# Attention after a long convolution: the residual added on VectorE, one paced list of background work, and two spectra loaded early

## The chip, the cores and the metric

The kernel runs on one core of a Trainium2 chip. The metric is device microseconds of one execution; the figure given is the median of several runs. TensorE (PE in the profile, with PEld for its weight loads) multiplies, VectorE (DVE), ScalarE (ACT) and GpSimd (POOL) work on elements, SyncE (SP) issues most DMAs. Matrix products land in PSUM and must be copied out by VectorE or ScalarE.

## What is computed

The state x has 2048 rows of 512 (bf16). Four layers follow each other, each on a layer norm of x and each added to x:

```
x = A_u
x = x + conv(layernorm(x))        # per channel: FFT convolution with a kernel made from the A, B, C parameters, plus a skip
x = x + attention(layernorm(x))   # 32 heads of 16; each row sees itself and 7 earlier rows, 2 apart
x = x + conv(layernorm(x))        # the same convolution
x = x + attention(layernorm(x))   # the same weights
```

The attention, cut to what matters:

```python
idx = pos[:, None] - arange(8)[None, :] * 2          # dilated window, masked where idx < 0
logits = einsum("bhsd,bhswd->bhsw", q, kg) * scale
o = einsum("bhsw,bhswd->bhsd", softmax(logits), vg)
return o.reshape(B, S, D) @ wo
```

## The kernel before, in words

**Stages.** `kernel_and_first_conv` builds the convolution's spectra, uses them for the first convolution and stores each of the four (one per 128 channels, 1 MB) to a DRAM scratch `kt_dram`. Then `b_layer` does the first attention, `a_layer` the second convolution, which loads the spectra `Kt` back (L731 to L734, two buffers), and `b_layer` the second attention, whose results go to the output. All share x as one tile `X` in SBUF.

**How the attention is tiled.** Since the window has a step of 2, even and odd rows are independent; `par` (0 or 1) names the half. With the half `fp` of the heads it makes four quarters, n = 2 par + fp. A quarter has two groups of 128 features, `f2` = 0 and 1, and nine blocks `b` of 114 queries (128 keys each).

- `start(g)` (L856): layer norm of four row slots on VectorE, transposes on PE, and four copies of the result from PSUM into `xnT` (L870, two on VectorE, two on ScalarE). Groups 0 and 1 make the even half, 2 and 3 the odd half.
- `proj(n, k)` (L875): one half (`h`) of the queries or keys of one `f2`: four matmuls of 512 columns, a copy to `st` (L886, VectorE for h = 0, ScalarE for h = 1) and, after the second half, two DMAs that spread `st` into a query or key set (`QS`, `KS`, L890). There are two pairs of sets, used by turns by the quarters. The order in k is f2, then query or key, then half: k = 0 to 3 is the whole of f2 = 0.
- `vproj(par, b)` (L892): the values of a block, four matmuls and a VectorE copy to `V` (L897).
- `logits(n, b)` (L899): 16 small matmuls for keys by queries of a block in two PSUM tiles `S4`, and two exponentials on ScalarE (L911) into one of three tiles `PT`.
- `values(n, b)` (L916): 16 matmuls of PT by V, whose extra column gives the sum; VectorE takes the reciprocal (L928) and multiplies (L930).
- `turn_o(n, b)` (L936): two transposes on PE; after every third block a VectorE copy to `oT` (L945).
- `out(m)` (L947): for one of 16 row slots four matmuls of `oT` by `wo` (L952), a fifth with the identity that adds the old x (L954), and a ScalarE copy to `X` (L955). After every fourth slot come the next layer norm's statistics (first attention: L202, L207 to L210 with a square root on ScalarE) or the store of the output (second attention).

The main loop (L974) takes t = 0 to 39. In step t it emits the logits of block t (t = 9 n + b), then background work, then the values of block t - 2, then the turn of block t - 4. The background work is: a value projection in the quarters n = 0 and 2, a projection of the next quarter's heads for b < 8 in n = 0, 1, 2, an `out` of the even rows for b < 8 in n = 3. All eight projections of quarter 0 are emitted before `start(2)` and the loop, the last eight outs after it.

All PSUM tiles but `S4` come from one pool of four (`psG`). The order in which an engine gets its instructions is that of a scheduler: it goes by the order of the code (with the earlier places that `at(tc, marks[..])` gives), and takes a later instruction when an earlier one isn't ready in its own reckoning. Waits are set from the data and buffers. Each engine then runs its list in order.

Of the kernel before, what the change touches and what calls it, by code (L numbers as in the profile page):

```python
# [11 lines left out]
ALU = mybir.AluOpType  # L12
AX = mybir.AxisListType
F32 = mybir.dt.float32
BF = mybir.dt.bfloat16
# [20 lines left out]
UF = 8  # L36
UP = UF + S // 2 + 16
NQ = 114
NB = 9
# [677 lines left out]
def a_layer(nc, tc, C, X, kt_dram, ln, ln_b, marks):  # L717

    with ExitStack() as es:
# [3 lines left out]
        kp = es.enter_context(tc.tile_pool(name="a_kt", bufs=2))  # L723
# [6 lines left out]
        Kt = []  # L730
        for dc in range(4):  # L731
            t = kp.tile([128, 4, 2, 512], BF, name="Kt", tag="Kt")
            nc.sync.dma_start(t[:], kt_dram[dc])
            Kt.append(t)  # L734
# [94 lines left out]
def b_layer(nc, tc, C, X, Wt, ln_b, marks, store=None, ln_next=None):  # L829

    with ExitStack() as es:
# [9 lines left out]
        oT = big.tile([128, 4, 2, QW], BF, name="oT")  # L841
# [14 lines left out]
        def start(g):  # L856
            par, j0 = g // 2, (g % 2) * 4
            xn = []
            for i in range(4):
                xn.append(xnp.tile([128, D], BF, name="xn", tag="xn"))  # L860
                ln_b.norm(xn[i][:], X[:, slot(g * 4 + i), :], g * 4 + i)
            for ch in range(2):
                pt = gps([128, 4, 2, 128], BF)
                for i in range(4):
                    for c in range(2):
                        ct = ch * 2 + c
                        nc.tensor.transpose(pt[:, i, c, :], xn[i][:, ct * 128:(ct + 1) * 128], ident[:])  # L867
                for c in range(2):
                    dst = xnT[:, ch * 2 + c, par, UF:UF + 1024].rearrange("c (p j) -> c p j", j=8)[:, :, j0:j0 + 4]
                    (nc.vector.tensor_copy if ch == 0 else nc.scalar.copy)(  # L870
                        dst, pt[:, :, c, :].rearrange("c j p -> c p j"))
# [3 lines left out]
        def proj(n, k):  # L875
# [10 lines left out]
            (nc.scalar.copy if h else nc.vector.tensor_copy)(st[n][:, h * 512:h * 512 + 512], ps[:])  # L886
# [12 lines left out]
        def logits(n, b):  # L899
            KS, QS = sets[n % 2]  # L900
            pt = PT[(n * NB + b) % 3]
            for ih in range(2):
                S4 = psS.tile([128, 2, 512], F32, name="S4", tag="S4")
                for sl in range(4):
                    f2, e = sl // 2, sl % 2
                    for ii in range(2):
                        r = slice(32 * (ih * 2 + ii), 32 * (ih * 2 + ii) + 32)
                        nc.tensor.matmul(S4[:, ii, sl * NQ:(sl + 1) * NQ], KS[r, e, f2, b * NQ + 1:b * NQ + 1 + NK],  # L908
                                         QS[r, e, f2, UF + b * NQ:UF + b * NQ + NQ],
                                         start=True, stop=True, skip_group_check=True)  # L910
# [3 lines left out]
        pts = {}  # L914

        def values(n, b):  # L916
            par, fp = n // 2, n % 2
            pt = PT[(n * NB + b) % 3]
            O = gps([128, 16, DH + 1])
            for i in range(4):  # L920
                for sl in range(4):
                    f2, e = sl // 2, sl % 2
                    c0 = (i * 4 + sl) * NQ
                    nc.tensor.matmul(O[:, f2 * 8 + i * 2 + e, :], pt[:, c0:c0 + 128],  # L924
# [7 lines left out]
            return on  # L932

        ons = {}

        def turn_o(n, b):  # L936
            par, fp = n // 2, n % 2
            if b % 3 == 0:
                pts[n] = gps([128, 3, 2, NQ], BF)
            on = ons.pop((n, b))  # L940
            for f2 in range(2):
                nc.tensor.transpose(pts[n][:, b % 3, f2, :], on[0:NQ, f2 * 128:(f2 + 1) * 128], ident[0:NQ, 0:NQ])  # L942
            if b % 3 == 2:
                dst = oT[:, fp * 2:fp * 2 + 2, par, (b - 2) * NQ:(b + 1) * NQ].rearrange("f t (b q) -> f t b q", q=NQ)
                nc.vector.tensor_copy(dst, pts[n][:].rearrange("f b t q -> f t b q"))  # L945

        def out(m):  # L947
            j = slot(m)
            par, jp = j % 2, j // 2
            ps = gps([128, 512])  # L950
            for ft in range(4):
                nc.tensor.matmul(ps[:], oT[:, ft, par, 0:1024].rearrange("f (p j) -> f j p", j=8)[:, jp],  # L952
                                 wo_t[:, ft, :], start=(ft == 0), stop=False)
            nc.tensor.matmul(ps[:], ident[:], X[:, j, :], start=False, stop=True)  # L954
            nc.scalar.copy(X[:, j, :], ps[:])  # L955
# [11 lines left out]
        for k in range(8):  # L967
            proj(0, k)
# [3 lines left out]
        todo = []  # L972
        LA, LT = 2, 4
        for t in range(4 * NB + LT):  # L974
            if t < 4 * NB:
                n, b = t // NB, t % NB
                logits(n, b)
                if n % 2 == 0:
                    vproj(n // 2, b)
                if n < 3 and b < 8:  # L980
                    proj(n + 1, b)
                if n == 3 and b < 8:
                    out(b)
            if t >= LA and t - LA < 4 * NB:
                n, b = (t - LA) // NB, (t - LA) % NB
                ons[n, b] = values(n, b)
            if t >= LT:
                turn_o((t - LT) // NB, (t - LT) % NB)
# [6 lines left out]
def kernel(  # L995
# [32 lines left out]
    marks = b_layer(nc, tc, C, X, Wt, ln_b, marks, ln_next=ln)  # L1028
    marks = a_layer(nc, tc, C, X, kt_dram, ln, ln_b2, marks)
# [33 lines left out]
```

## Time and profile before

| | |
|---|---|
| median of 4 runs (lowest to highest) | 587.9 us (582.4 to 589.48) |
| the profiled execution's own time | 587.12 us |
| its span | 585.3 us |
| busy: PE, DVE, ACT, POOL | 420.4, 425.6, 374.3, 17.9 us |
| first convolution with the spectra | to about 271 us |
| first attention | about 272 to 391 us |
| second convolution | about 390 to 461 us |
| second attention | about 461 to 585 us |
| granted TensorE clock, mean over the span | 0.9 |

A row of the timeline reads: start, duration, engine, line of the kernel, operation, written and read tiles with shapes, number of instructions merged; in brackets the idle time of the engine before it and what ended it. Durations of matmuls are modelled and overlap, so starts are the surer part. A shape such as 128x512 is partitions by elements.

### The profile page before, as it was taken

How to read it: one execution, taken by the hardware profiler on the slowest of the kernel's cores; microseconds unless marked ns; L12 is line 12 of the kernel's file. 1: busy time of each engine (PE TensorE's matmuls, PEld its weight loads, DVE VectorE, ACT ScalarE, POOL GpSimd, SP SyncE). 2: the span in 40 equal slices, each digit the busy share in tenths (PEclk: the TensorE clock that was granted, in tenths of full speed). 3: DMA queues.
4: the chain of work that ended last, by engine and by line, in shares of the span. 5: the costliest groups of instructions: out<-in, count | busy, mean ns of one | idle time of the engine just before them, and what ended most of it. 6: DMA issues, size and time to landing. Idle time of an engine off the chain costs nothing.

```text
span 585.3 us, 15269 instructions
## 1 busy us (share of the span) xinstructions
PE 420.4 (72%) x6522; PEld 261.4 (45%) x6522; DVE 425.6 (73%) x966; ACT 374.3 (64%) x511; POOL 17.9 (3%) x56
## 2 busy tenths in 40 slices
PE   1101576685684594636999999985997599989996
PEld 0101342462372363314455555643665445555573
DVE  5999999899999988336755565672999964545531
ACT  4999455363562453533488878954995448876793
POOL 0000000000000000321000000000000200000000
PEclk9999997796896887775999999996999789997999
DMA  8101146535535536571111110025661011111113
GB/s 291 76 1 36 25 106 90 107 112 109 93 120 109 69 122 130 125 197 73 73 47 47 56 56 20 3 91 125 173 175 14 1 73 42 52 56 37 39 46 101
DMA packets 80616, 48.57 MB, mean 83 GB/s; under 512 B 66723, under 2 KB 72740, under 8 KB 79268
## 3 DMA queue, kind: packets, MB, share of 16 engines
q1 hardware_dynamic: 77764, 42.75, 28.2%
q0 software_dynamic: 1200, 4.46, 2.7%
q8 instruction: 51, 0.84, 0.6%
q10 hardware_dynamic: 1584, 0.39, 0.3%
q14 instruction: 17, 0.14, 0.1%
HBM read 18.22 MB, written 8.39 MB: 45 GB/s over the span
## 4 chain that ended last, share of the span: by engine, by line
PE 35%; DVE 9%; ACT 7%; DMA 5%; issue 3%; SPq 0%; ACTq 0%; DVEq 0%
PE psG L884 10%; PE S L908 5%; PE psG L895 5%; PE psG L952 4%; PE psG L924 3%; ACT PT L911 3%; DMA zt<-Z 3%; DMA KS<-st 2%; DVE ln_st_b L202 2%; PE psG L867 1%; DVE pa L772 1%; DVE pb L773 1%; ACT xc L764 1%; PE psG L942 1%; PE psG L954 1%
## 5 line engine op out<-in xcount | busy, mean ns | idle before, releaser
L911 ACT ACTIVATE PT<-S 128x912 bf16<-128x912 f32 x144 | 126.4, 938 | 32.0 <-PE S L908 31.7
L884 PE MATMUL psG<-xnT,wqk 128*128 128x512 bf16 x256 | 70.6, 400 | 1.1 <-DVE xnT L870 1.1
L908 PE MATMUL S<-QS,KS 32*128 32x114 bf16 x1152 | 43.9, 213 | 5.8 <-DMA KS<-st 4.0
L928 DVE RECIPROCAL rd<-psG 114x16 f32<-114x16 f32 x72 | 18.2, 253 | 40.9 <-PE psG L924 40.9
L924 PEld LDWEIGHTS <-PT 128*128 128x128 bf16 x1152 | 39.2, 96 | 16.6 <-ACT PT L911 1.3
L897 DVE CAST V<-psG 128x512 bf16<-128x512 f32 x36 | 25.0, 694 | 24.3 <-PE psG L895 24.3
L924 PE MATMUL psG<-V,PT 128*128 128x17 bf16 x1152 | 41.0, 171 | 0.9 <-ACT PT L911 0.6
L254 PE MATMUL psA<-X,sb_F 128*128 128x128 bf16 x128 | 13.8, 242 | 36.4 <-ACT X L627 35.2
L895 PE MATMUL psG<-wv,xnT 128*128 128x512 bf16 x144 | 39.6, 389 | 0.0
L908 PEld LDWEIGHTS <-KS 32*128 32x128 bf16 x1152 | 26.1, 94 | 29.2 <-issue 16.1
L952 PE MATMUL psG<-wo_t,oT 128*128 128x512 bf16 x128 | 37.3, 400 | 0.3 <-DVE oT L945 0.2
L884 PEld LDWEIGHTS <-wqk 128*128 128x128 bf16 x256 | 23.5, 101 | 29.0 <-issue 5.1
L254 PEld LDWEIGHTS <-sb_F 128*128 128x128 bf16 x256 | 16.7, 105 | 42.7 <-issue 40.6
L886 DVE CAST st<-psG 128x512 bf16<-128x512 f32 x32 | 22.0, 687 | 17.0 <-PE psG L884 15.8
L272 PE MATMUL psA<-zt,sb_C 128*128 128x512 bf16 x30 | 15.2, 540 | 26.7 <-DMA zt<-Z 22.6
L241 ACT CAST Z<-psA 128x1024 bf16<-128x1024 f32 (+1 forms) x32 | 28.9, 977 | 7.1 <-PE psA L254 7.1
L584 PE MATMUL psk<-Ytab,Xtab 128*32 128x64 bf16 x1024 | 23.4, 205 | 12.9 <-issue 6.2
L930 DVE TENSOR_TENSOR on<-psG,rd 114x256 bf16<-114x256 f32 x72 | 30.1, 419 | 1.6
L587 PE MATMUL psk<-Y2tab,Xtab 128*32 128x48 bf16 x1024 | 22.5, 201 | 11.7 <-issue 9.9
L565 DVE TENSOR_TENSOR Ytab<-Ytab,MA 128x2048 bf16<-128x2048 bf16 (+1 forms) x33 | 30.6, 927 | 0.2
L567 DVE TENSOR_TENSOR Y2tab<-Ytab,MB 128x2048 bf16<-128x2048 bf16 (+1 forms) x33 | 30.5, 925 | 0.0
L241 ACT CAST xc<-psA 128x1024 bf16<-128x1024 f32 x16 | 15.7, 1014 | 22.4 <-PE psA L275 22.4
(183 smaller groups left out, 1013.4 us busy)
## 6 DMA issues: line engine op xcount, KB each, us to landing
kt_scratch<-Kt SPq DMA_DIRECT2D x4, 1024.0 KB, 3.9
QS<-st SPq DMA_DIRECT2D x32, 128.0 KB, 2.1
KS<-st SPq DMA_DIRECT2D x32, 128.0 KB, 2.1
Kt<-kt_scratch SPq DMA_DIRECT2D x4, 1024.0 KB, 5.9
X<-in_A_u_dram SPq DMA_DIRECT2D x4, 512.0 KB, 5.2
Xr<-in_A_u_dram SPq DMA_DIRECT2D x4, 512.0 KB, 4.7
out_dram<-X SPq DMA_DIRECT2D x4, 512.0 KB, 2.9
k_scratch<-KTq SPq DMA_DIRECT2D x7, 256.0 KB, 2.2
```

The lines of the kernel that those rows point to most:

```text
L241: self.nc.scalar.copy(dst, src)
L254: nc.tensor.matmul(o, F1[:, j, r, :], rhs_j(j), start=True, stop=not dk)
L565: nc.vector.tensor_tensor(v(Y[:, :, :, q * EYB:(q + 1) * EYB, :]), src, vm(self.mult(self.MA, lev, hc, EYB)), ALU.mult)
L567: nc.vector.tensor_tensor(v(Y2[:, :, :, (q - 1) * EYB:q * EYB, :]), src, vm(self.mult(self.MB, lev, hc, EYB)), ALU.mult)
L884: nc.tensor.matmul(ps[:], wqk[:, ct, f0:f0 + 128], xnT[:, ct, par, UF + h * 512:UF + h * 512 + 512], start=(ct == 0), stop=(ct == 3))
L895: nc.tensor.matmul(ps[:].rearrange("p h d -> p (h d)"), xnT[:, ct, par, NQ * b + 1:NQ * b + 1 + NK], wv[:, ct, :], start=(ct == 0), stop=( ...
L897: nc.vector.tensor_copy(V[:, par * NB + b, :, 0:DH], ps[:])
L908: nc.tensor.matmul(S4[:, ii, sl * NQ:(sl + 1) * NQ], KS[r, e, f2, b * NQ + 1:b * NQ + 1 + NK], QS[r, e, f2, UF + b * NQ:UF + b * NQ + NQ], ...
L911: nc.scalar.activation(pt[:, ih * 8 * NQ:(ih + 1) * 8 * NQ].rearrange("k (i x) -> k i x", i=2), S4[:, :, 0:4 * NQ], ACT.Exp, scale=DH ** -0.5)
L924: nc.tensor.matmul(O[:, f2 * 8 + i * 2 + e, :], pt[:, c0:c0 + 128], V[:, par * NB + b, (fp * 2 + f2) * 8 + i * 2 + e, :], start=True, stop ...
L930: nc.vector.tensor_tensor(on[0:NQ].rearrange("q (h d) -> q h d", d=DH), O[0:NQ, :, 0:DH], rd[0:NQ].unsqueeze(2).to_broadcast([NQ, 16, DH]) ...
L952: nc.tensor.matmul(ps[:], oT[:, ft, par, 0:1024].rearrange("f (p j) -> f j p", j=8)[:, jp], wo_t[:, ft, :], start=(ft == 0), stop=False)
```

## The change

In both attentions:

- A step t now takes two neighbouring blocks of one `f2` (over the nine steps of a quarter: the nine blocks of f2 = 0, then those of f2 = 1), where it took one block of both. The fifth step of a quarter has block 8 of f2 = 0 and block 0 of f2 = 1. `oT` is laid out by par first, and a turn writes one flat stretch of it.
- Only the first four projections (f2 = 0) stand before `start(2)`. The other 28 projections, the 18 value projections and the first eight outs, 54 pieces in all, form one list; a function `pace(t)` says how many of them are to be emitted by step t, linear between given points.
- `out`: 12 of 16 slots add the old x on VectorE from PSUM, without the fifth matmul. The odd ones of the last eight keep the matmul and the ScalarE copy.
- Copies to `st`: all on VectorE but those with h = 1 of quarter 0. Copies to `xnT`: groups 0 and 1 all on ScalarE; groups 2 and 3 half on each.

Around them: the pool of `Kt` is opened once, ahead of the first attention, and the loads of the first two spectra are emitted in the first attention at step 9. `a_layer` loads the other two.

```diff
-def a_layer(nc, tc, C, X, kt_dram, ln, ln_b, marks):
+def a_layer(nc, tc, C, X, kt_dram, kp, Kt, ln, ln_b, marks):
...
-        kp = es.enter_context(tc.tile_pool(name="a_kt", bufs=2))
...
-        Kt = []
-        for dc in range(4):
+        for dc in range(2, 4):
             t = kp.tile([128, 4, 2, 512], BF, name="Kt", tag="Kt")
             nc.sync.dma_start(t[:], kt_dram[dc])
             Kt.append(t)
...
-        oT = big.tile([128, 4, 2, QW], BF, name="oT")
+        oT = big.tile([128, 2, 4, QW], BF, name="oT")
...
-                    (nc.vector.tensor_copy if ch == 0 else nc.scalar.copy)(
+                    (nc.scalar.copy if par == 0 or c == 0 else nc.vector.tensor_copy)(
...
-            (nc.scalar.copy if h else nc.vector.tensor_copy)(st[n][:, h * 512:h * 512 + 512], ps[:])
+            (nc.scalar.copy if n == 0 and h == 1 else nc.vector.tensor_copy)(st[n][:, h * 512:h * 512 + 512], ps[:])
...
+        def logits(t):
+
+            KS, QS = sets[t // NB % 2]
+            pt = PT[t % 3]
             for ih in range(2):
                 S4 = psS.tile([128, 2, 512], F32, name="S4", tag="S4")
+                for x in range(2):
+                    f2, b = (t % NB * 2 + x) // NB, (t % NB * 2 + x) % NB
+                    for e in range(2):
+                        sl = x * 2 + e
...
+        def turn_o(t):
+            n, s = t // NB, t % NB
...
+            if s % 3 == 2:
+                dst = oT[:, n // 2, n % 2 * 2:n % 2 * 2 + 2, :].rearrange("f t q -> f (t q)")
+                nc.vector.tensor_copy(dst[:, (s - 2) * 2 * NQ:(s + 1) * 2 * NQ],
+                                      pts[n][:].rearrange("f b q -> f (b q)"))
 
         def out(m):
...
+            on_act = m >= 8 and m % 2 == 1
             for ft in range(4):
-                nc.tensor.matmul(ps[:], oT[:, ft, par, 0:1024].rearrange("f (p j) -> f j p", j=8)[:, jp],
-                                 wo_t[:, ft, :], start=(ft == 0), stop=False)
-            nc.tensor.matmul(ps[:], ident[:], X[:, j, :], start=False, stop=True)
-            nc.scalar.copy(X[:, j, :], ps[:])
+                nc.tensor.matmul(ps[:], oT[:, par, ft, 0:1024].rearrange("f (p j) -> f j p", j=8)[:, jp],
+                                 wo_t[:, ft, :], start=(ft == 0), stop=(ft == 3 and not on_act))
+            if on_act:
+                nc.tensor.matmul(ps[:], ident[:], X[:, j, :], start=False, stop=True)
+                nc.scalar.copy(X[:, j, :], ps[:])
+            else:
+                nc.vector.tensor_tensor(X[:, j, :], ps[:], X[:, j, :], ALU.add)
...
-        for k in range(8):
+        for k in range(4):
             proj(0, k)
         for g in range(2, 4):
             with at(tc, marks[g]):
                 start(g)
-        todo = []
+        queue = [lambda k=k: proj(0, k) for k in range(4, 8)]
+        queue += [lambda b=b: vproj(0, b) for b in range(NB)]
+        queue += [lambda k=k: proj(1, k) for k in range(8)]
+        queue += [lambda k=k: proj(2, k) for k in range(4)]
+        queue += [lambda b=b: vproj(1, b) for b in range(4)]
+        queue += [lambda k=k: proj(2, k) for k in range(4, 8)]
+        queue += [lambda b=b: vproj(1, b) for b in range(4, NB)]
+        queue += [lambda k=k: proj(3, k) for k in range(8)]
+        queue += [lambda m=m: out(m) for m in range(8)]
+        queue.reverse()
         LA, LT = 2, 4
+        done, N = 0, 4 * NB
+
+        def pace(t):
+
+            at_t = ((-1, 0), (3, 10), (8, 17), (17, 29), (26, 42), (31, 50))
+            for (a, x), (b, y) in zip(at_t, at_t[1:]):
+                if t <= b:
+                    return x + (y - x) * (t - a) // (b - a)
+            return len(queue) + done
+        for t in range(N + LT):
+            if t == NB and during is not None:
+                during()
+            if t < N:
+                logits(t)
+            want = pace(t)
+            while done < want:
+                queue.pop()()
+                done += 1
+            if LA <= t < N + LA:
+                values(t - LA)
             if t >= LT:
+                turn_o(t - LT)
         for m in range(8, 16):
             out(m)
...
+    kp = ctx.enter_context(tc.tile_pool(name="a_kt", bufs=2))
+    Kt = []
+
+    def early():
+        for dc in range(2):
+            t = kp.tile([128, 4, 2, 512], BF, name="Kt", tag="Kt")
+            nc.sync.dma_start(t[:], kt_dram[dc])
+            Kt.append(t)
+    marks = b_layer(nc, tc, C, X, Wt, ln_b, marks, ln_next=ln, during=early)
+    marks = a_layer(nc, tc, C, X, kt_dram, kp, Kt, ln, ln_b2, marks)
```

## The prediction

> **What bounds the kernel now.** I read the page's busy line first, then the stretches (busy time by window), then the timeline of the first attention step by step, then the waits and the rows of shapes for prices. The profiled execution took 587.12 us (span 585.3 and 1.8 around it); the median shown is 587.9, 0.8 more. The sum is made against 587.12, and 0.8 is put on at the end.
>
> The change touches only the two attentions. Their middle looks like this (columns: stretch, length, busy time of PE, PEld, DVE, ACT and POOL with counts, granted clock, DMA share, GB/s):
>
> ```profile
> 287.80:390.40 102.60, 99.25 (x1473) 58.14 (x1472) 60.18 (x150) 83.02 (x110) 0.00 (x0) 0.98 0.10 35
> 478.00:580.90 102.90, 99.10 (x1475) 57.84 (x1472) 48.46 (x116) 78.87 (x104) 0.00 (x0) 0.97 0.14 51
> ```
>
> TensorE reads busy nearly all the time, but its ends are modelled, so I price it from start to start. In the first quarter (n = 0), one step of the loop with two background items:
>
> ```profile
> 308.33 1.04 PE L895 MATMUL psG<-wv,xnT 128*128 128x512 bf16 x4
> 309.21 1.03 PE L884 MATMUL psG<-xnT,wqk 128*128 128x512 bf16 x4
> 310.07 0.55 PE L924 MATMUL psG<-V,PT 128*128 128x17 bf16 x16
> 310.48 0.26 PE L942 MATMUL psG<-sb_ident,on 114*128 114x114 bf16 x2
> 310.67 0.40 PE L908 MATMUL S<-QS,KS 32*128 32x114 bf16 x16
> ```
>
> The next step begins at 311.00, so a step is 2.67 us: 0.87 for each item (a projection or value projection, four matmuls) and 0.93 for values, turn and logits together. It repeats 2.67 with no gap: PE-bound. An `out` costs 0.87 and 0.22 for its residual matmul.
>
> The whole need of one attention from the first projection to the last `out`, at full clock: 36 steps x 0.93 = 33.5; 32 + 18 items x 0.87 = 43.5; 16 outs x 1.09 = 17.4; 32 transposes of the second half of x, 2.1 (rows of 1.50 and 0.62). Sum 96.5, and about 1.5 for the low clock at the start. It takes from 277.75 to 390.4 = 112.6 in the first attention, 467.07 to 580.8 = 113.7 in the second. So some 15 us in each are not PE work. ScalarE's rows show where:
>
> ```profile
> 321.63 0.59 ACT L886 CAST st<-psG 128x512 bf16<-128x512 f32 x1
> 322.13 1.75 ACT L911 ACTIVATE PT<-S 128x912 bf16<-128x912 f32 x2
> 324.06 1.75 ACT L911 ACTIVATE PT<-S 128x912 bf16<-128x912 f32 x2 [0.17 <-PE S L908]
> 325.70 0.59 ACT L886 CAST st<-psG 128x512 bf16<-128x512 f32 x1
> 326.19 1.75 ACT L911 ACTIVATE PT<-S 128x912 bf16<-128x912 f32 x2
> ...
> 330.26 1.75 ACT L911 ACTIVATE PT<-S 128x912 bf16<-128x912 f32 x2
> 333.97 3.40 ACT L911 ACTIVATE PT<-S 128x912 bf16<-128x912 f32 x4 [1.96 <-PE S L908]
> ```
>
> - Second quarter: a step is 2.03 (322.13 to 326.19 is two), though PE needs 0.93 + 0.87 = 1.80; ACT is full with two exponentials at 0.83 and half a copy. Lost 8 x 0.23 = 1.9.
> - Quarter ends: 311.15 to 314.29, 330.26 to 333.97 and 354.06 to 358.06 for steps whose PE work is 0.9 to 1.8: logits wait for keys that were projected just before and go to their set by DMA (the keys' store issued at 330.38, logits at 333.9, so 3.5 from issue). Lost about 5 for three, some of it filled by work pulled ahead.
> - Last quarter: 2.13 a step for 2.02 of PE, and the square root's table swap holds ACT from 368.43 to 371.81: about 4.
> - Start (logits at 287.8, first exponential at 292.25) about 2, end about 2.
>
> In the second attention there is no swap, but one quarter end is worse, with the clock down after it:
>
> ```profile
> 520.95 1.75 ACT L911 ACTIVATE PT<-S 128x912 bf16<-128x912 f32 x2
> 526.26 1.75 ACT L911 ACTIVATE PT<-S 128x912 bf16<-128x912 f32 x2 [3.55 <-PE S L908]
> 528.78 1.96 ACT L911 ACTIVATE PT<-S 128x912 bf16<-128x912 f32 x2 [0.77 <-PE S L908]
> ```
> ```profile
> 520.00:530.00 10.00, 8.38 (x116) 4.05 (x113) 4.46 (x10) 5.57 (x8) 0.00 (x0) 0.80 0.08 28
> ```
>
> From step 18 to step 21 it takes 9.25 (526.26 to 535.51) where the first attention takes 6.74: with 1.6 of longer wait, this hand-off cost 4.1 more than its twin.
>
> **The change part by part** (for each attention).
>
> *Residual.* 12 of 16 residual matmuls go: 12 x 0.22 = 2.6 off PE. 12 ScalarE copies (0.599) become VectorE adds. No such add is in the trace: at least 0.419 (the multiply from PSUM, 256 elements), at most twice 0.694; I take 0.69, the copy of 512 float32 from PSUM, the nearest row. DVE +8.3, ACT -7.2.
>
> *Evacuations.* 12 `st` copies go from ACT (0.591) to DVE (0.687): DVE +8.2, ACT -7.1. Four xnT copies go the other way (0.683 to 0.59). All four of each early group are then ACT's: 8 x 0.54 from 273.6 ends at 277.9, where the last copy now ends at 277.7, while DVE, for whose norms PE waits there, gets 1.3 free per group. Between +0.6 and -1.3; I take 0.
>
> *Order of heads and blocks, oT's layout.* The same instructions and sizes. The oT copy keeps 684 elements and I take its 0.46; a faster one, at least 0, would be off the path. Cost 0, hidden behind PE.
>
> *Balance.* In the loop DVE goes from 60.2 to about 77 of some 97 us, ACT from 83 to 69, PE needs 88 (36 x 0.93, 46 items x 0.87, 12 outs x 0.87, 4 x 1.09). PE stays the bound. Of a one-item step PE needs 1.80, two exponentials 1.65, DVE 0.83 + 0.69: PE-bound by little, where it was ACT-bound.
>
> *Pace.* The 46 items and 8 outs come as 10 in steps 0 to 3, then about 1.4 a step to step 31, 4 at step 32. Four projections leave the time before the first logits; they are its filler now. proj(0,3) ends at about 277.75 + 16 x 0.26 = 281.9; evacuation and DMA of 4.1 are covered by 2.1 of transposes and two items. Lost at the start 0.5 where it was 2.
>
> *The hand-offs are the wait that the change adds.* Logits 9 need proj(1,3), which the pace issues last in step 8; logits 27 need proj(3,3), last in step 26. Behind the waiting logits stand values, turns and more items on PE; ACT waits for them. Before, one step lay between. Step 18's keys come at step 14: no wait left. At least 0 (items without other needs are pulled ahead), at most the 5.8 of the worst row (1.7 and 4.1); I take 2, the ordinary end. Two: 4.
>
> *Step 31 on.* Steps 33 to 35 have no items: 3 x (1.65 - 0.93) = 2.2. In the first attention the eight outs' adds and statistics (0.69 + 0.69 + 0.17) are 12.4 on DVE beside 5.0 of its step work, in six steps where PE needs 12.5: 4.9 lost; two table swaps of 2.9 lie in the same time. I take 5 there, 2.2 in the second. End 2, as now; unevenness 0.5.
>
> *Early spectra.* Before, both loads issue at 390.28 and land in 5.9 each, while the first product runs at 412.60: hidden, so gain 0, at most 1.5 for the transposes at 400.62. Written at step 9, they are likely to go out earlier: a buffer's load is issued ahead of its line when its space is free (wq_in at 226.99, before the first convolution's last copies at 271), and SP issues nothing between 263.66 and 281.76. Cover is that empty stretch; if it is gone, a key store waits behind 2 x 5.9. I take 0.
>
> Sum, first attention: need 96.5 + 1.5 - 2.6 = 95.4; lost 0.5 + 4 + 5 + 2 + 0.5 = 12; 107.4 against 112.6, so 5.2 less. Second: 95.4 + 0.5 + 4 + 2.2 + 2 + 0.5 = 104.6 against 113.7, 9.1 less. Together 14.3: 587.1 - 14.3 = 572.8, and with 0.8: **574**.
>
> Two rules weighed. The row at 520 has the clock at 0.80 after a wait in which exponentials stood still for 3.55 and PE for less. The Trainium skill, "TensorE: Matmul & The Clock Gate", section on HAM oscillation, lets the clock fall only for PE gaps above about 3.4 us; by it four hand-offs of 2 would leave the clock alone and the sum stands, by the row they could cost 2.5 each on top, 584. Against the change speaks "DMA: Bandwidth & Descriptors", section Queues, rings and completion order: on each DMA engine descriptors are consumed in ring order, so stores behind the two loads wait for both. By that rule, loads issued just ahead of the first store would make 586; no run here shows a key store behind a load.
>
> **The rivals.**
> - *Hand-offs decide, the other side.* For it: the 5.8 row, and no free step of 1.8 now, so up to 7.6 each: 4 x (7.6 - 2) = 22 more, 596. Against: 40 items could be pulled ahead. Each above 5.5 eats the whole gain; above 7 it is slower than measurable. At 4 to 6.5: 582 to 592.
> - *VectorE becomes the bound.* For: 79% over the loop, four PSUM buffers that only it empties. Against: in the 2.67 steps DVE had vproj and half the projections already. If a tenth of 28 steps of 2.67 is lost in each attention, 2 x 7 = 14: 588; at half of that 581.
> - *The early loads delay keys.* 11.8 once: 574 + 11.8 = 586.
> - *Everything fills.* Hand-offs at 0 and nothing at step 31 in the first attention: 8 + 3 less: 563.
>
> **How the numbers follow.** Forecast (566 to 582) 0.55; everything fills 0.10; VectorE 0.10, half of it under 582; early loads 0.05; hand-offs 0.20, half of it above 594. A measurement of this kernel tells about 1% from no change, 582.0 and 593.8. Faster: 0.55 + 0.10 + 0.05 = 0.70; same: 0.05 + 0.05 + 0.10 = 0.20; slower 0.10. The range reaches from the filled case to the hand-offs at 6.5: 562 to 592.
>
> **What would show it.** Right: steps of 2.67 and 1.8 to 1.9 through all four quarters; logits near 286; step 27 to 36 without ACT copies; last `out` some 5 and 14 us earlier than 390 and 581. Wrong: exponentials more than 3.5 apart at steps 9 and 27, a clock under 0.9 inside a loop, PE waiting on DVE's psG releases, the spectra's loads between a projection's stores.

## The result, and the profile after

Over 53 runs the changed kernel takes 590.2 us (median), over 79 runs the kernel before 586.8: the ratio is 1.0043, 95% interval [1.0029, 1.0058]. The forecast had 574, a ratio of 0.976. The changed kernel is no faster, and by less than 1% slower. Its profiled execution took 589.12 us (span 587.0), 2.0 more than that of before.

The line of busy time says little; ScalarE has lost work (374.3 to 356.6) and VectorE has gained some (425.6 to 450.8), roughly as costed:

```profile
PE 423.6 (72%) x6498; PEld 264.7 (45%) x6498; DVE 450.8 (77%) x1006; ACT 356.6 (61%) x473; POOL 17.9 (3%) x56
```

Where the time went is read from segments, start to start (first matmul of a projection, end of the last `out`):

| segment | before | after | forecast |
|---|---|---|---|
| start to first projection, attention 1 | 277.75 | 280.67 (+2.9) | 0 |
| attention 1, to the last `out` | 112.6 | 114.2 (+1.6) | -5.2 |
| last `out` to the first transposing load of the convolution | 10.3 | 11.6 (+1.4) | 0 |
| that load to the first projection, attention 2 | 66.5 | 65.0 (-1.4) | 0 |
| attention 2, to the last `out` | 113.7 | 110.9 (-2.8) | -9.1 |
| end | 4.5 | 4.6 | 0 |

(Of the first 2.9, some 2.5 are there at 225 us, ahead of any edit: two executions differ by as much in the first convolution, where the granted clock from 60 to 130 us was 0.90 before and 0.78 after. What the edit did there is shown below by ratios.)

The two stretches of the attentions, first logits to last `out`, with the columns as before; DVE is up by 12 and 16, ACT down by 10 and 13:

```profile
289.20:394.85 105.65, 100.40 (x1469) 59.42 (x1468) 72.17 (x170) 73.26 (x87) 0.00 (x0) 0.95 0.10 37
480.95:582.43 101.48, 99.38 (x1467) 58.88 (x1466) 64.46 (x141) 66.11 (x78) 0.00 (x0) 0.97 0.15 54
```

Inside attention 1, ScalarE's timeline at step 9 and at step 27 (start, duration, merged count, idle before), then attention 2's step 9:

```profile
307.99 3.56 ACT L912 ACTIVATE PT<-S 128x912 bf16<-128x912 f32 x4 [1.39 <-PE S L909]
316.52 8.34 ACT L912 ACTIVATE PT<-S 128x912 bf16<-128x912 f32 x10 [4.97 <-PE S L909]
...
352.55 3.56 ACT L912 ACTIVATE PT<-S 128x912 bf16<-128x912 f32 x4 [1.39 <-PE S L909]
361.29 6.69 ACT L912 ACTIVATE PT<-S 128x912 bf16<-128x912 f32 x8 [5.19 <-PE S L909]
...
507.85 8.53 ACT L912 ACTIVATE PT<-S 128x912 bf16<-128x912 f32 x10 [4.97 <-PE S L909]
```

ScalarE stands still for about 5 us each time. In that gap SP issues the keys' store and the first logits follow 2.6 us behind it:

```profile
309.64 1.10 SPq L888 DMA_DIRECT2D QS<-st  x2
312.76 1.10 SPq L888 DMA_DIRECT2D KS<-st  x2
```
```profile
315.08 0.38 PE L882 MATMUL psG<-xnT,wqk 128*128 128x512 bf16 x1
315.40 0.23 PE L909 MATMUL S<-QS,KS 32*128 32x114 bf16 x4
```

PE does not stand still: it runs projections and values ahead, and the clock stays at 1.00 there (third-last column):

```profile
312.00:316.00 4.00, 4.00 (x70) 2.39 (x65) 3.78 (x10) 0.00 (x0) 0.00 (x0) 1.00 0.18 66
```

Afterwards ScalarE is what is full: from step 9 on ten exponentials stand without a gap, at 1.62 to 1.64 us a step. PE's recorded waits for them are short, 0.31 behind each hand-off. (`PE S L909 <- ACT PT L912` adds up to 3.5 us in attention 1, but 2.6 of that stands at the table swaps, which come next.)

The second place is the end of attention 1. ScalarE swaps its table four times between exponentials:

```profile
373.03 1.28 ACT L208 ACT_TABLE_LOAD   x1
...
375.73 1.28 ACT L912 ACT_TABLE_LOAD   x1 [1.11 <-PE S L909]
377.03 0.93 ACT L912 ACTIVATE PT<-S 128x912 bf16<-128x912 f32 x1
377.98 1.28 ACT L208 ACT_TABLE_LOAD   x1
...
379.58 1.28 ACT L912 ACT_TABLE_LOAD   x1
```

and TensorE's clock goes down to a half in the stretches (third-last column) that follow:

```profile
370.00:374.00 4.00, 4.00 (x49) 2.67 (x48) 4.00 (x12) 3.02 (x4) 0.00 (x0) 1.00 0.00 0
374.00:378.00 4.00, 2.68 (x72) 2.20 (x71) 4.00 (x13) 2.85 (x5) 0.00 (x0) 1.00 0.02 6
378.00:382.00 4.00, 1.78 (x25) 1.03 (x26) 2.70 (x13) 3.96 (x5) 0.00 (x0) 0.54 0.00 0
382.00:386.00 4.00, 4.00 (x62) 2.61 (x59) 1.36 (x4) 3.12 (x4) 0.00 (x0) 0.50 0.01 4
```

The third place is ahead of the attention. The spectra's loads were issued at 254.22, ahead of every key store, so no key waits behind them. But their two buffers take space that other tiles had. GpSimd's fill of `V`, which stood at 263.21 before, now waits for space until 273.51 (the norm's row of the kernel before is put ahead of the two after):

```profile
273.51 2.52 POOL L845 MEMSET V<- 128x576 bf16 x1
```
```profile
271.51 1.31 DVE L213 TENSOR_SCALAR xn<-X,ln_rstd_b,ln_nb_b 128x512 bf16<-128x512 bf16 x4
```
```profile
273.99 3.34 DVE L213 TENSOR_SCALAR xn<-X,ln_rstd_b,ln_nb_b 128x512 bf16<-128x512 bf16 x4
277.66 1.37 DVE L213 TENSOR_SCALAR xn<-X,ln_rstd_b,ln_nb_b 128x512 bf16<-128x512 bf16 x4
```

The first four norms of the attention take 3.34 where the same four took 1.31 before and the next four take 1.37. The 2.03 more is what was left of the fill when the first norm came (276.03 - 273.99 = 2.04). The Trainium skill, "SBUF — State Buffer", section Who interferes with whom, says that VectorE in a two-port mode and GpSimd exclude each other for whole instructions, and that a `tensor_scalar` can enter such a mode when its operands allow it. The rows agree: the norms are `TENSOR_SCALAR`, and the first of the four ends at 276.23, just behind the fill.

### The profile page after: what moved, and what is told of

It is laid out like the page before. It is cut to its first block, busy times and chain, and to the rows that moved or that the text cites. A ratio compares the mean times of both kernels' runs of the same rounds, so it can differ in the third digit from the quotient of the medians.

```text
span 587.0 us, 15149 instructions
## 1 busy us (share of the span) xinstructions
PE 423.6 (72%) x6498; PEld 264.7 (45%) x6498; DVE 450.8 (77%) x1006; ACT 356.6 (61%) x473; POOL 17.9 (3%) x56
## 4 chain that ended last, share of the span: by engine, by line
PE 34%; DVE 10%; ACT 7%; DMA 4%; issue 3%; SPq 0%; ACTq 0%; DVEq 0%
PE psG L882 9%; PE S L909 6%; PE psG L956 5%; PE psG L893 5%; PE psG L926 4%; ACT PT L912 4%; DMA zt<-Z 3%; DVE ln_st_b L202 2%; PE psG L865 1%; DVE pa L770 1%; PE psG L944 1%; DVE pb L771 1%; ACT xc L762 1%; PE ps_s L743 1%; DVE VT L793 1%
## 5 line engine op out<-in xcount | busy, mean ns | idle before, releaser
L912 ACT ACTIVATE PT<-S 128x912 bf16<-128x912 f32 x144 | 124.6, 936 | 51.9 <-PE S L909 48.1
L882 PE MATMUL psG<-xnT,wqk 128*128 128x512 bf16 x256 | 67.5, 386 | 1.5 <-ACT xnT L868 1.4
L884 DVE CAST st<-psG 128x512 bf16<-128x512 f32 x56 | 38.6, 690 | 25.5 <-PE psG L882 24.9
L909 PE MATMUL S<-QS,KS 32*128 32x114 bf16 x1152 | 46.9, 213 | 6.2 <-ACT PT L912 4.6
L926 PE MATMUL psG<-V,PT 128*128 128x17 bf16 x1152 | 42.5, 171 | 0.2
L909 PEld LDWEIGHTS <-KS 32*128 32x128 bf16 x1152 | 27.7, 94 | 29.5 <-issue 23.5
L893 PE MATMUL psG<-wv,xnT 128*128 128x512 bf16 x144 | 37.5, 382 | 0.0
L956 PE MATMUL psG<-wo_t,oT 128*128 128x512 bf16 x128 | 35.7, 416 | 0.0
L241 ACT CAST Z<-psA 128x1024 bf16<-128x1024 f32 (+1 forms) x32 | 28.8, 979 | 7.2 <-PE psA L254 7.2
L882 PEld LDWEIGHTS <-wqk 128*128 128x128 bf16 x256 | 22.2, 99 | 24.0 <-issue 3.9
L587 PE MATMUL psk<-Y2tab,Xtab 128*32 128x48 bf16 x1024 | 22.1, 200 | 11.5 <-issue 9.7
L316 DVE TENSOR_TENSOR pa<-xc,Kt 128x1024 bf16<-128x1024 bf16 x16 | 11.0, 690 | 22.4 <-ACT Kt L241 12.3
```

Source lines behind the costliest of these rows:

```text
L241: self.nc.scalar.copy(dst, src)
L882: nc.tensor.matmul(ps[:], wqk[:, ct, f0:f0 + 128], xnT[:, ct, par, UF + h * 512:UF + h * 512 + 512], start=(ct == 0), stop=(ct == 3))
L884: (nc.scalar.copy if n == 0 and h == 1 else nc.vector.tensor_copy)(st[n][:, h * 512:h * 512 + 512], ps[:])
L893: nc.tensor.matmul(ps[:].rearrange("p h d -> p (h d)"), xnT[:, ct, par, NQ * b + 1:NQ * b + 1 + NK], wv[:, ct, :], start=(ct == 0), stop=( ...
L909: nc.tensor.matmul(S4[:, i, sl * NQ:(sl + 1) * NQ], KS[r, e, f2, b * NQ + 1:b * NQ + 1 + NK], QS[r, e, f2, UF + b * NQ:UF + b * NQ + NQ], ...
L912: nc.scalar.activation(pt[:, ih * 8 * NQ:(ih + 1) * 8 * NQ].rearrange("k (i x) -> k i x", i=2), S4[:, :, 0:4 * NQ], ACT.Exp, scale=DH ** -0.5)
```

## The experiments

Each ratio is to the kernel before, with its 95% interval; the changed kernel has 1.0043.

### The hand-offs: two steps of lead, one step, three steps

```diff
-            at_t = ((-1, 0), (3, 10), (8, 17), (17, 29), (26, 42), (31, 50))
+            at_t = ((-1, 0), (3, 10), (6, 17), (17, 29), (24, 42), (31, 50))   # e1_handoff
+            at_t = ((-1, 0), (3, 10), (7, 17), (17, 29), (25, 42), (31, 50))   # e6_lead1
+            at_t = ((-1, 0), (3, 10), (5, 17), (17, 29), (23, 42), (31, 50))   # e10_lead3
```

> Only the pace differs from the changed kernel: 17 pieces by step 6 (was step 8) and 42 by step 24 (was 26), so that proj(1,3) and proj(3,3) come two steps before the logits that need them. In the changed kernel the exponentials stand still for 4.97 before step 9 and 5.19 before step 27, in both attentions. Theory hand-off: the gaps fall under 1.5 and each hand-off gives 2 to 4 back, 8 to 14 us in all: 0.976 to 0.986 of the changed kernel, 0.981 to 0.991 of the kernel before. Rival, TensorE is full anyway (it worked ahead during the gaps and ScalarE only catches up after them): the gaps go, the time stays within 2 us. Rival, the wait moves: it appears at another step with the same length.

Measured: 0.9848 [0.9813, 0.9883].

> The changed kernel with the keys' last projection one step ahead of its logits (17 by step 7, 42 by step 25), between the changed kernel (none between, ratio 1.0043) and the run with two steps (0.9848). Theory hand-off: store to logits takes 3.5 after a copy of 0.7, a two-piece step is 2.67, so one step covers about two thirds: gaps of 1.5 to 3 before steps 9 and 27 and a ratio of 0.988 to 0.995. Rival, any step between suffices: 0.985. Rival, the gain was from how the pieces lie and not from the lead: 1.0.

Measured: 0.9927 [0.9894, 0.9959].

> The changed kernel with three steps of lead at the two hand-offs in each attention; it had none (1.004), with one step 0.993, with two 0.985. Theory 1 (two steps hide the whole way of the keys from the store to the logits, about 3.5 us against steps of 1.8 to 2.7): nothing more to gain, 0.982 to 0.988. Theory 2 (each step of lead is worth about 5 us still): 0.975 to 0.980. Theory 3 (items moved earlier make the steps before the hand-off longer and leave fewer for the steps after it): 0.988 to 0.995.

Measured: 0.9841 [0.9795, 0.9887].

The time falls with each step of lead up to two and no further: 1.0043, 0.9927, 0.9848, 0.9841. With two steps, ScalarE's timeline of attention 1 shows a wait of 0.58 at step 9 (313.78) where it had 4.97, and none of PE for keys. The 1.78 two steps earlier is what the three items of step 6 leave it (3.53 from exponential to exponential, 2.67 + 0.87 of PE). In attention 2 PE still waits 0.51 for the keys of step 9 (last row):

```profile
306.11 1.75 ACT L912 ACTIVATE PT<-S 128x912 bf16<-128x912 f32 x2 [0.92 <-PE S L909]
309.64 3.56 ACT L912 ACTIVATE PT<-S 128x912 bf16<-128x912 f32 x4 [1.78 <-PE S L909]
313.78 3.61 ACT L912 ACTIVATE PT<-S 128x912 bf16<-128x912 f32 x4 [0.58 <-PE S L909]
```
```profile
500.09 0.72 PE L909 MATMUL S<-QS,KS 32*128 32x114 bf16 x16 [0.51 <-DMA KS<-st]
```

So the four hand-offs cost 0.0195 of 588 us, about 11.5 us, 2.9 each. Without them the change is a gain of 1.5%.

### The early spectra, and the fill that they moved

`e2_late_kt` opens the pool and loads all four spectra in the second convolution, as before. `e14_memset` keeps the early loads and lets VectorE fill `V`'s column of ones behind the first four projections:

```diff
-        nc.gpsimd.memset(V[:, :, :, DH], 1.0)
...
         for k in range(4):
             proj(0, k)
+        nc.vector.memset(V[:, :, :, DH], 1.0)
...
```

> The changed kernel with the spectra loaded as before (pool and loads inside the second convolution). Theory: the early pool pushed the attention's tiles 16 KB up, so GpSimd's memset of V came at 273.5 instead of 263.2 and held one layer norm of VectorE for 2 us ahead of the first projection; undone, the norm is 1.3 to 1.4 again, the memset is back near 263, and the time is 2 us less (0.9965 of the changed kernel). Rival: the loads were worth something in the second convolution: 0 to 1.5 us more. Rival: neither shows, 0.

Measured: 0.9987 [0.9953, 1.0021].

> The changed kernel with the early spectra as they are, and only V's column of ones set by VectorE after the first four projections, where GpSimd set it at 273.5 us beside VectorE's norms. Theory 1 (the early loads cost time only because their space pushes that GpSimd fill onto the norms, 3.34 for four where 1.31 is usual): the norms take 1.31 again, the first projection comes about 2 us earlier, ratio to before 0.998 to 1.001 where the changed kernel had 1.004. Theory 2 (the loads, the later first projection and the fill are not linked so; the space itself or the loads cost it): 1.003 to 1.006.

Measured: 0.9999 [0.9968, 1.0030]. The norms are back:

```profile
274.01 1.35 DVE L213 TENSOR_SCALAR xn<-X,ln_rstd_b,ln_nb_b 128x512 bf16<-128x512 bf16 x4
```

Moving the fill alone is worth 0.0044, 2.6 us; taking the early loads out altogether gives no more that these intervals could tell. So no gain from the loads is seen, and as far as the intervals tell, their cost is the fill that their space displaced.

### The residual: back on TensorE and ScalarE, and alone in the kernel before

```diff
-            on_act = m >= 8 and m % 2 == 1
+            on_act = True                      # e3_res_pe
```

> The changed kernel with the residual as before: the fifth matmul and the ScalarE copy for all 16 outs. Theory VectorE at the end: in the first attention from step 30 on VectorE is full (10.00 of 10 in 370 to 380) with adds and statistics; undone, the first attention's end is 2 to 4 shorter and the second's 1 to 2 longer (12 matmuls of 0.22 are back on TensorE): together 0 to 3 less. Rival, the residual matmuls were a true 2.6 on the bound: 3 to 5 us more than the changed kernel.

Measured: 1.0118 [1.0080, 1.0156].

> The kernel before with the residual part of the change alone: 12 of 16 outs without the fifth matmul, added by VectorE. Theory: it is a gain by itself, since the last quarter's steps are bound by ScalarE (2.13 for two exponentials and a copy): 8 steps of 2.13 go to 1.8 to 1.9 in both attentions and the last eight outs lose 4 x 0.22: 2.5 to 3.5 each, ratio 0.988 to 0.992. Rival, VectorE's adds and statistics hold the first attention's end: only the second gains, 0.994 to 0.997.

Measured: 0.9997 [0.9964, 1.0030], a miss of both expectations. The add on VectorE is worth 0.0075 (4.4 us) in the changed kernel, where the sum had 2 x 2.6, and nothing by itself. In the profile of `e7_before_res` the stretch from step 27 to the last `out` gains in attention 2 (26.5 us for 28.8 before) and loses in attention 1 (35.5 for 32.3), where the granted clock falls as low as 0.57; one execution doesn't show whether the edit brings that.

### The copies: `st` on ScalarE again, and xnT's copies alone in the kernel before

```diff
-            (nc.scalar.copy if n == 0 and h == 1 else nc.vector.tensor_copy)(st[n]...
+            (nc.scalar.copy if h else nc.vector.tensor_copy)(st[n]...                  # e8_st_act
```
```diff
-                    (nc.vector.tensor_copy if ch == 0 else nc.scalar.copy)(
+                    (nc.scalar.copy if par == 0 or c == 0 else nc.vector.tensor_copy)( # e15_before_xnt
```

> The changed kernel with the copies to st as before (ScalarE for every second half). Theory: 24 copies on ScalarE make one-piece steps ScalarE-bound again, 12 x 0.2 in each attention, 2 to 5 us more: 1.008 to 1.013 of the kernel before. Rival, VectorE with its 79% was late for PSUM and is relieved: 1.000 or less. Where the hand-off waits decide, neither engine matters: 1.003 to 1.005.

Measured: 1.0103 [1.0054, 1.0153].

> The kernel before with one part of the change alone: the copies of the transposed x of an attention's first batch all on ScalarE. Theory 1 (what the profile of the changed kernel shows in the second attention, 65.0 for 66.5 from the first transposing load to the first projection): VectorE's norms no longer wait for copies, 1.4 us less in each attention, ratio 0.994 to 0.996. Theory 2 (the prediction's value, nothing: ScalarE's eight copies end when the mixed ones did): 0.999 to 1.001.

Measured: 0.9943 [0.9912, 0.9975]. Both parts of the change are gains: 0.6% each.

### The end of the attention: a late norm, one square root, the outs spread

`e4_defer` emits the next layer norm of the first eight slots behind slot 11. `e5_combo` has two steps of lead, the spectra loaded late, and one square root for the first twelve slots. `e9_spread` is that with the last point of the pace at step 35:

```diff
-            at_t = ((-1, 0), (3, 10), (6, 17), (17, 29), (24, 42), (31, 50))
+            at_t = ((-1, 0), (3, 10), (6, 17), (17, 29), (24, 42), (35, 54))
```

> The changed kernel with the square roots (and what follows them) of the next layer norm's first eight slots emitted after slot 11 instead of after slots 3 and 7, statistics as they were. Theory table swaps: in the first attention two swaps there and back (373.0 to 377.0 and 378.0 to 380.9) hold the last exponentials, after which the clock falls to 0.57; without them the last exponentials end 4 to 6 earlier and the first attention is 3 to 5 shorter. Rival, VectorE is what holds the end: under 1 us. The norms that wait for these roots can't start before the last out in either case, so no loss is expected above 1 us.

Measured: 0.9994 [0.9961, 1.0026]. Of the two pairs of swaps between the exponentials one goes (the other stands at 373.67 and 376.33 in this run's trace). It is worth 0.5%, 2.9 us, where 3 to 5 had been expected; from the first exponential of step 32 to the last it now takes 10.2 us where it took 12.9.

> The changed kernel with three things together: keys two steps ahead (17 pieces by step 6, 42 by step 24), the spectra loaded as before, and one square root for the first twelve slots of the next layer norm after slot 11, so that no table swap can come before the last exponentials. If the three costs are apart, their savings add: 0.985 of the kernel before for the first alone, less 0.0056 for the loads (1.0043 to 0.9987) and 0.005 to 0.008 for the swaps (0.9994 had taken one of two away): 0.971 to 0.976. Rival, they hide behind each other (VectorE at the first attention's end bounds it with or without swaps): 0.980 to 0.985.

Measured: 0.9792 [0.9750, 0.9833]. Between the two expectations, of parts that add up and of parts that hide each other. In its timeline the four outs of step 32 hold ScalarE up:

```profile
364.61 1.75 ACT L914 ACTIVATE PT<-S 128x912 bf16<-128x912 f32 x2 [0.97 <-PE S L911]
369.17 3.40 ACT L914 ACTIVATE PT<-S 128x912 bf16<-128x912 f32 x4 [2.81 <-PE S L911]
```

> The combined kernel (two steps of lead at each hand-off, spectra loaded late, one square root for the first twelve blocks), with one more number changed: the eight outs of the first batch come about one a step over steps 28 to 35, where four of them stood at step 32. In the combined kernel's profile ScalarE waits 2.81 us for the logits behind these four outs in the first attention, and the steps 33 to 35 have no item and so cost 0.23 to 0.7 each more of ScalarE than PE needs. Theory 1 (PE is idle for lack of items at the end): 2 to 4 us less in each attention, a ratio to the kernel before of 0.966 to 0.973 where the combined one had 0.979. Theory 2 (what is left at the end is VectorE's adds and statistics, the same number in any order): within 1 us of the combined kernel, 0.977 to 0.981.

Measured: 0.9674 [0.9635, 0.9713], 568.5 us: the fastest of the complete kernels here. TensorE's clock is 1.00 from the first logits to the last `out` of attention 1:

```profile
285.00:380.40 95.40, 93.53 (x1471) 57.03 (x1469) 71.12 (x167) 68.68 (x81) 0.00 (x0) 1.00 0.11 41
```

From the first exponential of step 32 to the last one it takes 7.2 us in both attentions; the changed kernel takes 12.9 and 8.9.

### The step of 2.03: items between the halves, and half an exponential

In the forecast a step with one item went from 2.03 (ScalarE full with half a copy beside its exponentials) to 1.80 (TensorE's need). In the changed kernel ScalarE has no such copies, and wherever nothing else disturbs them two steps still take 4.06. TensorE's timeline of `e9_spread` shows every second set of logits lengthened:

```profile
313.69 0.45 PE L911 MATMUL S<-QS,KS 32*128 32x114 bf16 x16
314.07 1.04 PE L884 MATMUL psG<-xnT,wqk 128*128 128x512 bf16 x4
...
315.55 0.80 PE L911 MATMUL S<-QS,KS 32*128 32x114 bf16 x16
...
317.75 0.45 PE L911 MATMUL S<-QS,KS 32*128 32x114 bf16 x16
318.13 1.04 PE L884 MATMUL psG<-xnT,wqk 128*128 128x512 bf16 x4
```

while ScalarE in the same steps waits 0.45 after every fourth exponential. Both engines wait, each for the other. `e11_split` (from `e5_combo`) and `e12_split_spread` (from `e9_spread`) write the step's items between the halves of its logits:

```diff
-                logits(t)
+                logits(t, (0,))
             want = pace(t)
             while done < want:
                 queue.pop()()
                 done += 1
+            if t < N:
+                logits(t, (1,))
```

> The combined kernel, with the step's background items written between its two halves of logits and exponential, not behind both. A one-item step takes 2.03 us in every kernel so far, whether ScalarE has copies in it (before) or none (changed), where PE needs 1.80 and two exponentials 1.65; in the profile the second half's logits wait about 0.4 us for the tile that the exponential still holds. Theory 1 (PE and ScalarE wait for each other in turn over the two tiles of logits, since both halves stand side by side on PE): with 0.87 us of other work between the halves the wait goes, steps of 1.80 to 1.87, some 15 such steps in each attention: 5 to 7 us less, a ratio of 0.967 to 0.971 where the combined kernel had 0.979. Theory 2 (the 0.23 is the price of passing a tile between the engines, or PE's own, and stays in any order): 0.977 to 0.981.

Measured: 1.0012 [0.9979, 1.0045].

> Both at once: the outs of the first batch spread over steps 28 to 35, and the items between the two halves of logits. If both are gains of their own: the sum of the two steps, 0.954 to 0.965. If both only fill the same idle time at the end of the attention: the better of the two, 0.966 to 0.973. If neither has an effect: 0.977 to 0.981.

Measured: 0.9949 [0.9917, 0.9982]. Both far outside every expectation, 2.2% and 2.8% slower than their parents. TensorE's timeline of `e11_split`:

```profile
311.20 1.04 PE L884 MATMUL psG<-xnT,wqk 128*128 128x512 bf16 x4
312.17 0.37 PE L911 MATMUL S<-QS,KS 32*128 32x114 bf16 x8
312.47 0.56 PE L928 MATMUL psG<-V,PT 128*128 128x17 bf16 x16
312.89 0.26 PE L946 MATMUL psG<-sb_ident,on 114*128 114x114 bf16 x2
313.08 0.37 PE L911 MATMUL S<-QS,KS 32*128 32x114 bf16 x8
313.39 1.04 PE L884 MATMUL psG<-xnT,wqk 128*128 128x512 bf16 x4
```

Start to start, each half of eight matmuls takes 0.30, together 0.61, where the sixteen side by side took 0.33 (the rows of the prediction, 310.67 to 311.00); the item takes 0.97 where it took 0.87. A step is 2.19, all of it TensorE's own. The halves read different rows of the sets (the slice `r` in `logits`: 0 to 63 and 64 to 127), so they can overlap only when they stand together; the Trainium skill, "TensorEngine Tiling (Array Packing)", section Key Properties, says that tiles of the array work independently and in parallel, which agrees. This run could not tell what the 0.23 is: it took one wait away and put a larger price in its place. So the other side of the pair was shortened: `e13_half_exp` is `e9_spread` with half of each softmax left out.

```diff
-                nc.scalar.activation(pt[:, ih * 8 * NQ:(ih + 1) * 8 * NQ].rearrange("k (i x) -> k i x", i=2),
-                                     S4[:, :, 0:4 * NQ], ACT.Exp, scale=DH ** -0.5)
+                nc.scalar.activation(pt[:, ih * 8 * NQ:(ih + 1) * 8 * NQ].rearrange("k (i x) -> k i x", i=2)[:, :, 0:2 * NQ],
+                                     S4[:, :, 0:2 * NQ], ACT.Exp, scale=DH ** -0.5)
...
-                    c0 = (i * 4 + sl) * NQ
+                    c0 = i * 4 * NQ
```

> The spread kernel (0.967), with each exponential taken over half of its logits and the values read from that half alone; TensorE's instructions stay the same in number and size, so half of the softmax is left out and only the time is read. A one-item step takes 2.03 us where TensorE's parts add up to 1.80. Theory 1 (each second step's logits wait some 0.4 us because the exponential, 0.83 long, still holds the tile): with exponentials of about 0.45 the tile is free in time, one-item steps take 1.80 to 1.85, some 20 of them in each attention: 8 to 10 us less in all, a ratio to the kernel before of 0.949 to 0.956. Theory 2 (the 0.23 is TensorE's own or the price of each hand-over between the engines): the steps stay at 2.0, ratio 0.964 to 0.970.

Measured: 0.9550 [0.9512, 0.9588]. No second set of logits is long any more:

```profile
315.55 0.40 PE L911 MATMUL S<-QS,KS 32*128 32x114 bf16 x16
315.88 1.04 PE L884 MATMUL psG<-xnT,wqk 128*128 128x512 bf16 x3
...
317.36 0.40 PE L911 MATMUL S<-QS,KS 32*128 32x114 bf16 x16
...
319.17 0.40 PE L911 MATMUL S<-QS,KS 32*128 32x114 bf16 x16
```

Steps of 1.81. The 0.23 is the wait for a tile of logits that the exponential still holds. In the spread kernel it costs 0.0124, 7.3 us (with these intervals, 4 to 11); in the two profiles, the steps 4 to 30 of both attentions take 7.1 less together.

## Why the prediction was wrong, point by point

The forecast was 0.976 and the result 1.0043: 0.028, or 16.4 us, too low. The direction was wrong, because a gain of 14 was summed from a need of TensorE and a few waits, and several terms failed the same way. The result lies inside the band that the hand-off rival spans (582 to 592), but that is luck: the hand-offs cost 2.9 each and not the rival's 4 to 6.5, and the rest of the miss came from other terms.

Most of it can be read in one stretch: from the first exponential of step 4 to that of step 31. It has 27 steps and 38 items, by the prediction's prices 27 x 0.93 + 38 x 0.87 = 58.2 us. The forecast added 4 for two hand-offs and 0.5. In the profiles (one execution each):

| kernel | attention 1 | attention 2 | over the need, together |
|---|---|---|---|
| forecast | 62.7 | 62.7 | 9.0 |
| changed kernel | 68.0 | 68.3 | 19.9 |
| with two steps of lead (`e1_handoff`) | 62.6 | 64.4 | 10.6 |
| with the rest mended too (`e9_spread`) | 62.7 | 63.7 | 10.1 |
| and half exponentials (`e13_half_exp`) | 59.0 | 60.4 | 3.0 |

The exponentials between which it is read in attention 1, in the changed kernel and in `e13_half_exp`:

```profile
300.52 2.74 ACT L912 ACTIVATE PT<-S 128x912 bf16<-128x912 f32 x3 [2.05 <-PE S L909]
368.54 1.75 ACT L912 ACTIVATE PT<-S 128x912 bf16<-128x912 f32 x2 [0.56 <-PE S L909]
```
```profile
301.15 0.99 ACT L914 ACTIVATE PT<-S 128x456 bf16<-128x456 f32 x2 [2.43 <-PE S L911]
360.13 0.99 ACT L914 ACTIVATE PT<-S 128x456 bf16<-128x456 f32 x2 [0.86 <-PE S L911]
```

(Four kernels with the changed kernel's loop agree within 0.03 us in attention 1; in attention 2 they take 68.3 to 72.1, so its column is the weaker one.) So 10.9 of the 16.4 us lie here. Without the hand-offs 9.3 of the 19.9 are gone, without the wait for the tile another 7.1.

- **The step that failed by most: "Of a one-item step PE needs 1.80, two exponentials 1.65 ...: PE-bound by little, where it was ACT-bound."** The step stayed at 2.03. The need of 95.4 counts every such step at 1.80. The row of 2.03 had been read as ScalarE being full; ScalarE was emptied and the step did not move. Here two engines that are each nearly full and pass two tiles to and fro add waits of their own, which neither engine's need shows. Price, from `e13_half_exp`: 7.3 us in the spread kernel, taken as 0. That is the price once the hand-offs are gone; in the changed kernel fewer steps show it, since ScalarE catches up behind each hand-off at 1.62 a step (in attention 1 the steps 16 and 19 take 2.25 beside 1.81).
- **The hand-offs.** The place, the mechanism and the filling by items pulled ahead were right, and the sign named for it, exponentials more than 3.5 apart at steps 9 and 27, is there; at 2 each they were too cheap. They cost 2.9 each, 11.5 for four instead of 8. That is 3.5 of the miss; but it is the term that decides between gain and loss. It did so below the 5.5 each that the rival gave as its threshold, since the rest of the gain was smaller than summed. The clock stayed at 1.00 there, where PE had other work.
- **The early spectra.** Right that they go out early and delay no key. Missed: their buffers take space, and what then moves. 2.6 us.
- **The copies to xnT.** Taken as 0 from bounds of +0.6 and -1.3 a group; alone on the kernel before they gain 0.0057, 3.4 us. This made the result better than the sum.
- **Step 31 on.** 5 and 2.2 were forecast as lost; by the time from step 32's first exponential to the last (12.9 - 7.2 and 8.9 - 7.2) it is 5.7 and 1.7 more than in `e9_spread`. The size was right. Of the cause, VectorE's adds (4.9 of the 5), the rows show VectorE full from 370 to 378; but one pair of swaps alone is worth 0.5% (`e4_defer`). What was not foreseen is how cheaply it goes: by one number of the pace and one square root.
- **The residual and `st`.** The add was estimated at 0.69 from the eviction row and has a mean of 0.675. The residual's gain is 4.4 for a forecast of 5.2. VectorE became no bound of the loop: in attention 1 PE's own waits for it add up to 0.9 us, both of them at the end, where it is full.
- **The start.** From the first projection to the first logits 8.6 us where it was 10.0; 1.5 had been forecast as gained. But in attention 1 two projections fewer stand there than before (24 matmuls for 32, 1.7 us of work), so the waits ahead of the first logits did not shrink.

Added up in this order: 7.3 + 3.5 + 2.6 - 3.4 = 10.0 of the 16.4. The rest, about 6, is not separated. Part of it lies in the need itself: in `e13_half_exp`, where hand-offs, swaps and long logits are gone, first projection to last `out` is 102.2 and 99.4, and the sum without these terms would be 98.4 (95.4, and 3.0 for start, end and unevenness).

Of the rivals, "hand-offs decide" had the right place and too high a price, "VectorE becomes the bound" and "early loads delay keys" did not occur, and "everything fills" (563) is near what the repaired kernel does (568.5), for other reasons.

Left open: the last 6 us; and whether a third tile of logits would free the one-item step (not tried).

## What to carry to other kernels

When a step is a few per cent longer than the need of its fullest engine, look at every second occurrence of the instructions at the hand-over before calling one engine the bound: two engines that share two buffers can each wait for the other, and emptying one of them a little need not shorten the step. When work is paced evenly, put the deadline of what the next stage loads (projection, copy, DMA, first use) into the pace; two steps of lead took 2% off here. When a tile is allocated earlier, look up what moves in its place, fills by GpSimd above all, and what runs on VectorE at that moment.

## What the runs showed of the hardware that was not expected

- Sixteen matmuls of 32 rows over four row groups take 0.33 us side by side, and 0.30 + 0.31 when other matmuls stand between the halves; the projection between them takes 0.97 for 0.87.
- TensorE's clock fell to a half behind short pauses. In attention 1 of the changed kernel PE works without a gap up to 376, then come gaps of 1.33 and 0.42 us; the clock is 1.00 until 378, 0.64 in the next microsecond and 0.50 after it. In attention 2 of the kernel before, one gap of 1.51 ends at 525.22, and from 526 the clock is 0.50. The Trainium skill, "TensorE: Matmul & The Clock Gate", section on HAM oscillation, names gaps above about 3.4 us. Here the measurement decides: 1.3 to 1.5 us were enough. In the changed kernel the pause comes with the table swaps, so the low clock is probably a part of what they cost; in attention 1 of `e9_spread`, without them and with the outs spread, it stays at 1.00.

```profile
378.01 0.38 PE L909 MATMUL S<-QS,KS 32*128 32x114 bf16 x8 [1.33 <-ACT PT L912]
378.80 0.37 PE L944 MATMUL psG<-sb_ident,on 114*128 114x114 bf16 x2 [0.42 <-DVE on L932]
```
```profile
378.00:379.00 1.00, 0.58 (x10) 0.34 (x9) 1.00 (x8) 1.00 (x1) 0.00 (x0) 0.64 0.00 0
379.00:380.00 1.00, 0.69 (x11) 0.32 (x9) 1.00 (x5) 0.97 (x3) 0.00 (x0) 0.50 0.00 0
```
```profile
525.22 0.23 PE L908 MATMUL S<-QS,KS 32*128 32x114 bf16 x4 [1.51 <-DMA KS<-st]
```
```profile
525.00:526.00 1.00, 0.78 (x10) 0.30 (x10) 0.00 (x0) 0.00 (x0) 0.00 (x0) 1.00 0.00 0
526.00:527.00 1.00, 1.00 (x23) 0.77 (x24) 0.92 (x3) 0.74 (x1) 0.00 (x0) 0.50 0.00 0
```

- A GpSimd fill of one column in 17 (2.52 us) held VectorE's norms for all of its remaining 2.04 us.
